# Attention and two feed-forward layers on one core: the second group's sums moved to VectorE, value products by two chunks of keys, and new planning numbers

## Chip, cores and metric

One core of a Trainium2 chip runs the whole kernel. The metric is the time of one execution on the device, in microseconds (us); the value given for a kernel is the median of several runs. Engines are named as the profile names them: PE is TensorE (PEld its loading of weights), DVE is VectorE, ACT is ScalarE, POOL is GpSimd, SP is SyncE, which issues the transfers.

## What is computed

Everything is float32. Four batches of 12 heads, 448 positions, 64 numbers a head; then two feed-forward layers over the 1792 rows that the heads give.

```python
q_n, k_n = rmsnorm(q, g_q), rmsnorm(k, g_k)
scores = (q_n @ k_n.T) / sqrt(64)
attn = exp(scores - max(scores)); attn = attn / (sum(attn) + 1e-9)
x = (attn @ v), heads side by side            # 1792 x 768
x = ((x @ w_a) * (x @ w_b)) @ w_out           # 768 -> 1536 -> 768
h = x @ w_in                                  # 768 -> 2048
out = (h * clip(h + 3, 0, 6) / 6) @ w_out2    # 2048 -> 768
```

## The kernel before

**Precision.** A large product is made of three: each operand is split into a high part, rounded to the fast type `float32r` by ACT, and a low part, the difference, made by DVE or POOL (`sub`, line 397). `tri` (line 690) issues high x high, high x low and low x high. The products of 448 columns at lines 691 to 693 (first group) and 964 (second group) are nearly all of PE's work.

**Attention** works on pairs of heads (`pair`, line 418). Scores come in seven chunks of 128 queries (lines 533 and 534), are reduced and exponentiated into seven tiles `p`, and are transposed back by blocks (lines 571, 585 to 588) into a buffer `pt`, of which there are two. The keys have four chunks for a pair of heads; for each chunk `k` one value step (`value`, line 596, product at 598) multiplies the transposed block with v for both heads and adds into one PSUM bank. Chunk 3 holds the last 64 keys of both heads, so its operands have another shape than those of chunks 0 to 2.

**Feed-forward** is done in two groups of two batches. The first group (batches 0 and 1) runs through `layer` while attention of batches 1 to 3 goes on beside it, to about 790 us in the profile. Weights are unpacked there by DVE and split by ACT and by POOL or DVE (`piece`, line 663). The second group (batches 2 and 3) runs through `layer7` (line 878), twice, once for each layer. It cuts each product of matrices into 2 x 2 blocks and needs seven block products instead of eight, at the price of sums: sums of weight blocks (`Left.sum`, line 921), the low parts of weights (`halve`, line 896), sums of activation blocks and their low parts (`Right`, line 1024), and the gate of the first layer (`gate`, line 1011). Results are added up out of PSUM by DVE (`take`, line 968). `x_maker` (line 826) prepares the activations at the start of either layer.

**The order of the work** is planned when the program is built. Each operation is added with a due time in a planned clock and with the engines that may do it, each with an estimated duration (`Plan.add`, line 166). `Plan.run` goes through planned time: each free engine takes the operation that is due first and whose inputs and buffers are there; one that may go to a second engine goes there if the first is busy for longer than `LW` or the operation is late. So the numbers at the top of the file set the order: `T` and `TQ` place the batches of attention, `R` the start and pace of each feed-forward layer, `O*` the offsets inside a pair of heads, `LW7`, `LX7`, `XLEAD`, `XSTEP` those of the second group, `LB`, `LF`, `LW` when an operation may go to another engine. On the chip each engine runs its own list in order and waits where an input is late.

```python
        vg, gv = {"V": (on_dve(PH), True), "G": on_pool(PH)}, {"G": on_pool(PH), "V": (on_dve(PH), True)}
            add(at(u + OD[1]), {"PE": 930}, value, reads=[(pt, 0), (pt, 1), rv], writes=[pv])
```

The first line (885) lets weight sums of the second group go to DVE ("V") or POOL ("G"), each with its cost in ns; the second (601) adds one value step.

Of the kernel before, what the change touches and what calls it, by code (L numbers as in the profile page):

```python
# [19 lines left out]
NB, NH, S, D = 4, 12, 448, 64  # L20
# [5 lines left out]
PH = DM // 2  # L26
# [1 line left out]

T = (6.793, 78.0, 255.0, 440.0)
TQ = (1.45, 3.637, 4.75, 4.118)
R = ((85.0, 1.515), (255.0, 1.267), (411.278, 1.34), (703.581, 1.0), (943.0, 1.0))


BS = ((2, 3, 4), (1, 2, 3, 4), (2, 3, 4), (3, 4))
# [18 lines left out]

LB = (
    (548.658, 276.261, 561.206), (548.658, 402.965, 561.206), (548.658, 402.965, 561.206),
    (735.919, 402.965, 561.206),  # L60
)
LF = (
    (548.658, 402.965, 561.206), (548.658, 402.965, 561.206), (548.658, 402.965, 561.206),
    (548.658, -149.766, 561.206),
)
LW = 112.877


OA = (-7.027, -5.631, -5.6, -5.526, -4.903, -4.8, -4.475, -4.381)
OB = (-4.0, -2.7, -3.2, -2.3, -2.579, -2.6, -2.385)  # L70
OC = (0.0, -0.24, 0.482, 0.457, 4.632, 4.519)
UT = 5.13
UK = 2.0
OD = (0.4, 1.972, 3.0)


LEAD = 21.868
OW = (-9.089, -9.23, 1.129, 3.002, -1.607)
AFTER = 2.571


SLICE = (3, 3, 2)
# [4 lines left out]


MM = 206.7
LW7 = (34.0, 25.0, 20.0, 18.0)  # L90

SLICE7 = ((3, 3), (3, 3, 2))
XLEAD, XSTEP = -14.0, 3.7
LX7 = (20.0, 19.0, 18.5)


def piece_order(up, down, n, k):
# [49 lines left out]
class Plan:  # L149
# [16 lines left out]
    def add(self, due, cost, fn, reads=(), writes=(), after=()):  # L166


        o = Op()
        o.due, o.fn, o.idx = due * 1000.0, fn, len(self.ops)  # L170
        o.late = self.late
        o.cost = {e: c if isinstance(c, tuple) else (c, e == "G") for e, c in cost.items()}
        o.succ, o.need, o.ready = [], 0, 0.0
        o.bufs = []
        deps = {id(d): d for d in after}
        for k in reads:
            if k in self.last:
                deps[id(self.last[k])] = self.last[k]
        for k in writes:
            if k in self.last:  # L180
                deps[id(self.last[k])] = self.last[k]
            for d in self.readers.pop(k, ()):
                deps[id(d)] = d
        for k in reads:
            self.readers.setdefault(k, []).append(o)
        for k in writes:
            self.last[k] = o
        seen = set()
        for k in (*reads, *writes):
            b = k[0] if isinstance(k, tuple) else k  # L190
            if isinstance(b, Buf) and id(b) not in seen:
                seen.add(id(b))
                o.bufs.append(b)
                b.left += 1
        deps.pop(id(o), None)
        for d in deps.values():
            d.succ.append(o)
        o.need = len(deps)
        self.ops.append(o)
        return o  # L200
# [103 lines left out]
def on_dve(n):  # L304
    return 66 + 1.043 * n
# [4 lines left out]


def on_pool(n):
    return (146 + 2.11 * n, True)


@with_exitstack
def fused_kernel(ctx: ExitStack, tc: tile.TileContext, nat, qt, gs_in, wpk, outT):
    nc = tc.nc
    V, A, G, SP = nc.vector, nc.scalar, nc.gpsimd, nc.sync
# [11 lines left out]
    def f32(ap):  # L331
        return ap.bitcast(F32)
# [57 lines left out]
    def bank(role, ids, ordered=True):  # L390
        return Buf([banks[i] for i in ids], lines.setdefault(role, []) if ordered else None)

    plan = Plan()
    add = plan.add

    def sub(e, out, a, b):
        e.tensor_tensor(out=out, in0=a, in1=b, op=ALU.subtract)  # L397
# [20 lines left out]
    def pair(n0):  # L418
# [6 lines left out]
        lower, upper = slice(0, D), slice(D, P)  # L425

        def at(u):
            return t0 + q * u

        def at_chunk(j):  # L430
# [4 lines left out]
        rn, rv, sq, kc, ms, rstd, nt, sums, rs = [  # L435
            buf(k) for k in ("rn", "rv", "sq", "kc", "ms", "rstd", "nt", "sums", "rs")]
# [5 lines left out]
        for i, (lo, hi, who) in enumerate(alike):  # L442
            add(at(-10.7 + i), {"SP": 90 * (hi - lo)}, lambda e, lo=lo, hi=hi: e.dma_start(
                out=rn.t[:, lo:hi].rearrange("p c d -> p (c d)"), in_=nat[n0 // 2][:, lo * D:hi * D]),
                writes=[(rn, k) for k in who])
        for i in range(2):
            add(at(-8.9 + (4 * i if n0 else 0)), {"SP": 640}, lambda e, i=i: e.dma_start(out=rqs[i].t, in_=qt[n0 + i]),
                writes=[rqs[i]])
        add(at(-2.0), {"SP": 640}, lambda e: e.dma_start(
            out=rv.t.rearrange("p c d -> p (c d)"), in_=nat[n0 // 2][:, 14 * D:]), writes=[rv])  # L450
        for i, (lo, hi, who) in enumerate(alike):
            n, sl = (hi - lo) * D, slice(lo, hi)
            x, y, z, m, sk = [[(o, k) for k in who] for o in (rn, rstd, nt, ms, sq)]

            def square(e, sl=sl):
# [5 lines left out]
            cost = {"V": (on_dve(n), True), "A": on_act(n), "G": on_pool(n)}  # L461
            add(at(OA[0]), {k: cost[k] for k in ("VAA"[i] if n0 == 0 else SQ[b])}, square,
                reads=x, writes=sk)
            add(at(OA[1]), {"V": on_dve(n)}, lambda e, sl=sl: e.reduce_sum(out=ms.t[:, sl], in_=sq.t[:, sl], axis=AX.X),
                reads=sk, writes=m)
# [3 lines left out]
                reads=m, writes=y)  # L469
            add(at(OA[4]), {"A": 100}, lambda e, sl=sl: e.activation(rstd.t[:, sl], rstd.t[:, sl], AF.Exp, scale=-0.5),  # L470
                writes=y)
# [85 lines left out]
        for j in range(0 if LATE[b] else NCK):  # L557
            opts = {"V": (363, True), "G": (617, True), "A": 560}
            add(at(4 + OC[5] + 0.15 * j), {k: opts[k] for k in NORM[b][j // 2]}, lambda e, j=j: norm(e, j),
                reads=[rs], writes=[ps[j]])  # L560
        pv = bank("v", BV[b])
        for k in range(4):
            pt = buf("pt")
            u = 4 + UT + k * UK
            if k < 3:
                for i, n in enumerate((4, 3)):
                    t = bank("t", BT[b], False)

                    def turn_p(e, k=k, i=i, n=n, t=t):
                        for c in range(n):  # L570
                            e.transpose(t.t[:, c * P:(c + 1) * P], ps[4 * i + c].t[:, k * P:(k + 1) * P], ident)  # L571

                    add(at(u + 0.5 * UK * i), {"PE": 109 * n}, turn_p, writes=[t, (pt, i)],
                        reads=["ident", *ps[4 * i:4 * i + n]])
                    cost = copy_ps(n * P)
                    add(at(u + 0.5 * UK * i + OD[0]), {x: cost[x] for x in PT[b]}, lambda e, i=i, n=n, t=t, pt=pt: copy(
                        e, pt.t[:, 4 * P * i:(4 * i + n) * P], t.t[:, :n * P]), reads=[t], writes=[(pt, i)])
                own = slice(0, P), slice(0, P)
                at_v, cols = (k, 4 + k), (0, S)
            else:  # L580
                t = bank("t", BT[b], False)

                def turn_rest(e, t=t):
                    for c in range(4):
                        e.transpose(t.t[:, c * P:(c + 1) * P], ps[3 + c].t[:, S - P:], ident)
                    for c in range(3):
                        e.transpose(t.t[lower, c * P:(c + 1) * P], ps[c].t[:, S - D:], ident)  # L587
                    e.transpose(t.t[lower, 3 * P:S], ps[3].t[lower, S - D:], ident[lower, lower])

                add(at(u), {"PE": 820}, turn_rest, reads=["ident", *ps], writes=[t, (pt, 0)])  # L590
                cost = copy_ps(4 * P)
                add(at(u + OD[0]), {x: cost[x] for x in PT[b]}, lambda e, t=t, pt=pt: copy(
                    e, pt.t[:, :4 * P], t.t), reads=[t], writes=[(pt, 0)])
                own, at_v, cols = (lower, upper), (3, 3), (0, D)

            def value(e, k=k, pt=pt, own=own, at_v=at_v, cols=cols):
                for i, rows in enumerate((lower, upper)):
                    e.matmul(pv.t[rows, :S], rv.t[own[i], at_v[i]], pt.t[own[i], cols[i]:cols[i] + S],  # L598
                             start=k == 0, stop=k == 3)

            add(at(u + OD[1]), {"PE": 930}, value, reads=[(pt, 0), (pt, 1), rv], writes=[pv])
        m, due = h // 2, at(u + OD[2])
        if LATE[b]:
            rb, eb = bank("t", BT[b], False), buf("tmp", "e")
# [273 lines left out]
    def layer7(no, ids, clock, late, finish):  # L878
# [3 lines left out]
        n = LAYERS[no][2] // 2  # L882
        now = dict(sevens)
        sevens.clear()
        vg, gv = {"V": (on_dve(PH), True), "G": on_pool(PH)}, {"G": on_pool(PH), "V": (on_dve(PH), True)}

        def mbank():
            return bank("m", ids)
# [120 lines left out]
            return t  # L1009

        def gate(c, ap, due, in_psum, b):
            cost = {"V": 535} if in_psum else {"V": (535, True), "G": on_pool(S)}
            add(due, cost, lambda e: e.tensor_tensor(out=b.t, in0=ap(), in1=b.t, op=ALU.mult), reads=[c], writes=[b])
            return b

# [8 lines left out]
        class Right:  # L1024
# [6 lines left out]
            def __call__(self, name, due):  # L1031
                x11, x12, x21, x22 = self.x
                if name == "t1":
                    self.minus(x12, x12, x11, due - LX7[0])
                if name == "t3":
                    self.minus(x11, x22, x11, due - LX7[0])
                c = {"b11": x11, "t1": x12, "b22": x22, "b21": x21, "t2": x22, "t3": x11, "t4": x21}[name]
                a = buf("act")
                add(due - LX7[1], {"A": 467}, lambda e: e.activation(a.t[:, 0], c.t, AF.Copy), reads=[c], writes=[(a, 0)])
                add(due - LX7[2], {"V": (535, True), "G": on_pool(S)}, lambda e: sub(e, a.t[:, 1], c.t, f32(a.t[:, 0])),  # L1040
                    reads=[c, (a, 0)], writes=[(a, 1)])
                if name == "b22":
                    self.minus(x22, x22, x12, due - LX7[2])
                if name == "b21":
                    self.minus(x21, x21, x22, due - LX7[2])
                return a

            def minus(self, to, x, y, due):
                add(due, {"V": (535, True), "G": on_pool(S)}, lambda e: sub(e, to.t, x.t, y.t),
                    reads=[z for z in (x, y) if z is not to], writes=[to])  # L1050

        def down(pairs, first, last):
# [128 lines left out]
```

## Time and profile before

| | |
|---|---|
| median of 3 runs | 1277.68 us (1277.48 to 1277.71) |
| the profiled execution | 1274.44 us |
| its span, first to last instruction | 1272.7 us |
| PE busy | 1236.0 us (97%) |
| DVE busy | 1027.8 us (81%) |
| ACT busy | 668.9 us (53%) |
| POOL busy | 258.0 us (20%) |

The profile records one execution. The 1.7 us between the profiled execution and its span lie before the first and behind the last instruction. Times inside the trace count from the start of the span. A matmul in the trace is shown with a modelled end, and consecutive ones overlap; the cost of one is read from start to start.

### The profile page before, as it was taken

To read this page: it belongs to the slowest core of one execution; us is meant where nothing else is said; L and a number is where in the kernel's file an instruction comes from. 1 tells how busy PE (TensorE), PEld (TensorE's weight loads), DVE (VectorE), ACT (ScalarE), POOL (GpSimd) and SP (SyncE) were. 2 spreads that over 40 slices of the span, in tenths; PEclk is the share of its full clock that TensorE was granted. 3 is DMA by queue.
4 is the path that set the end of the run, shared out by engine and by line. 5 is a ranking of instruction groups with operands and counts; after the bars stand their busy time and mean duration, and the time that the engine had idled before them with its cause. 6 is when DMAs were issued, how large, how long until landed. Compare 5 with 4: busy or idle time off the path is not lost.

```text
span 1272.7 us, 18366 instructions
## 1 busy us (share of the span) xinstructions
PE 1236.0 (97%) x6342; PEld 1039.3 (82%) x6342; DVE 1027.8 (81%) x1859; ACT 668.9 (53%) x1428; POOL 258.0 (20%) x281
## 2 busy tenths in 40 slices
PE   5999999999999999999999999999999999899998
PEld 3668777777988887888778878899899888799897
DVE  8999998997557798877878775876877799977977
ACT  7996766677235564654767643522422245534432
POOL 4331102212000021110121000522212234413131
PEclk9999999999999999999999999999999999999999
DMA  6456676765687587656646353655355445255433
GB/s 203 139 187 227 215 257 203 281 228 197 216 274 241 173 314 252 207 177 227 205 142 209 122 173 108 232 155 162 121 176 158 132 129 182 85 178 157 131 107 123
DMA packets 107853, 235.57 MB, mean 185 GB/s; under 512 B 9200, under 2 KB 74096, under 8 KB 107760
## 3 DMA queue, kind: packets, MB, share of 16 engines
q1 hardware_dynamic: 107760, 234.39, 56.2%
q8 instruction: 50, 0.82, 0.3%
q14 instruction: 43, 0.35, 0.1%
HBM read 162.01 MB, written 72.35 MB: 184 GB/s over the span
## 4 chain that ended last, share of the span: by engine, by line
PE 73%; DVE 15%; DMA 5%; issue 4%; ACT 2%; POOL 1%; SPq 0%; DVEq 0%; POOLq 0%; ACTq 0%
PE bank L964 26%; PE bank L691 10%; PE bank L693 10%; PE bank L692 10%; PE bank L598 5%; PE bank L571 4%; DMA wst<-in_w_dram 3%; PE bank L533 3%; PE bank L534 2%; DVE act L397 2%; DVE w L397 2%; DMA rn<-in_nat_dram 1%; PE bank L498 1%; DVE wf L649 1%; DVE acc L972 1%
## 5 line engine op out<-in xcount | busy, mean ns | idle before, releaser
L691 PE MATMUL bank<-xx,w 128*128 128x448 f32 x480 | 182.3, 380 | 1.1 <-DVE act L397 0.9
L693 PE MATMUL bank<-xx,w 128*128 128x448 f32 x480 | 175.5, 366 | 0.0
L692 PE MATMUL bank<-xx,w 128*128 128x448 f32 x480 | 175.4, 365 | 0.0
L964 PE MATMUL bank<-act,w 128*128 128x448 f32 x711 | 155.0, 366 | 6.0 <-DVE acc L972 4.1
L964 PEld LDWEIGHTS bank<-act,w 128*128 128x128 f32 x711 | 133.0, 188 | 18.9 <-ACT w L899 4.4
L964 PE MATMUL bank<-xx,w 128*128 128x448 f32 x612 | 132.1, 366 | 0.8 <-DVE acc L972 0.8
L691 PE MATMUL bank<-act,w 128*128 128x448 f32 x336 | 127.7, 380 | 2.6 <-DVE act L397 1.9
L673 ACT ACTIVATE w<-wf 128x768 fp32r<-128x768 f32 x104 | 85.6, 840 | 78.9 <-PE bank L692 64.8
L964 PEld LDWEIGHTS bank<-xx,w 128*128 128x128 f32 x612 | 114.9, 188 | 10.8 <-DVE acc L972 1.2
L693 PE MATMUL bank<-act,w 128*128 128x448 f32 x336 | 122.8, 366 | 0.0
L692 PE MATMUL bank<-act,w 128*128 128x448 f32 x336 | 122.7, 365 | 0.0
L397 DVE TENSOR_TENSOR w<-wf,w 128x384 fp32r<-128x384 f32 x185 | 101.3, 584 | 18.9 <-ACT w L673 15.8
L797 DVE TENSOR_TENSOR acc<-bank,acc 128x448 f32<-128x448 f32 x120 | 74.3, 622 | 48.4 <-PE bank L693 48.0
L539 DVE TENSOR_REDUCE nm<-bank 128x1 f32<-128x448 f32 x168 | 102.4, 618 | 13.0 <-PE bank L534 8.3
L543 ACT ACTIVATE p<-bank,nm,rstd 128x448 f32<-128x448 f32 x131 | 94.5, 724 | 27.5 <-PE bank L587 17.0
L408 ACT ACTIVATE pt<-bank 128x512 f32<-128x512 f32 (+1 forms) x131 | 71.4, 547 | 61.7 <-PE bank L571 51.4
L397 POOL TENSOR_TENSOR w<-wf,w 128x384 fp32r<-128x384 f32 x48 | 55.0, 1154 | 230.4 <-ACT w L673 224.8
L691 PEld LDWEIGHTS bank<-xx,w 128*128 128x128 f32 x480 | 90.2, 188 | 12.6 <-DVE act L397 1.7
L693 PEld LDWEIGHTS bank<-xx,w 128*128 128x128 f32 x480 | 90.1, 188 | 7.7
L692 PEld LDWEIGHTS bank<-xx,w 128*128 128x128 f32 x480 | 90.4, 188 | 6.2
L598 PE MATMUL bank<-pt,rv 128*64 128x448 f32 (+1 forms) x384 | 92.5, 563 | 0.5 <-DVE act L397 0.5
L964 PE MATMUL bank<-xt,w 128*128 128x448 f32 x405 | 89.7, 368 | 3.1 <-DVE xf L412 3.1
(214 smaller groups left out, 2487.4 us busy)
## 6 DMA issues: line engine op xcount, KB each, us to landing
wst<-in_w_dram SPq DMA_DIRECT2D x68, 768.0 KB, 5.9
split<-w SPq DMA_DIRECT2D x102, 384.0 KB, 3.7
w<-split SPq DMA_DIRECT2D x85, 384.0 KB, 3.9
kept<-wf SPq DMA_DIRECT2D x68, 384.0 KB, 3.0
wf<-kept SPq DMA_DIRECT2D x65, 384.0 KB, 4.2
wst<-kept SPq DMA_DIRECT2D x39, 384.0 KB, 3.6
rq<-in_qt_dram SPq DMA_DIRECT2D x48, 224.0 KB, 3.4
rn<-in_nat_dram SPq DMA_DIRECT2D x23, 448.0 KB, 4.1
```

What stands on the lines that cost most here:

```text
L397: e.tensor_tensor(out=out, in0=a, in1=b, op=ALU.subtract)
L408: A.activation(out, in_, AF.Copy)
L539: add(at(u + OC[1]), {"V": 531}, lambda e, s=s, nm=nm: e.tensor_reduce(out=nm.t, in_=s.t[:, :S], axis=AX.X, op=ALU.max, negate=True), read ...
L543: add(at(u + OC[3]), {"A": 704}, lambda e, j=j, s=s, nm=nm, p=p: e.activation(p.t, s.t[:, :S], AF.Exp, bias=nm.t, scale=rstd.t[:, qcol[j]: ...
L571: e.transpose(t.t[:, c * P:(c + 1) * P], ps[4 * i + c].t[:, k * P:(k + 1) * P], ident)
L598: e.matmul(pv.t[rows, :S], rv.t[own[i], at_v[i]], pt.t[own[i], cols[i]:cols[i] + S], start=k == 0, stop=k == 3)
L673: add(due - LEAD + OW[2], {"A": on_act(DM)}, lambda e: e.activation(w.t[:, 0], wf.t.bitcast(F32), AF.Copy), reads=both, writes=[(w, 0, 0), ...
L691: e.matmul(ps, w.t[:, 0, wsl], xh, start=start, stop=False)
L692: e.matmul(ps, w.t[:, 0, wsl], xl, start=False, stop=False)
L693: e.matmul(ps, w.t[:, 1, wsl], xh, start=False, stop=stop)
L797: add(due, {"V": 535}, lambda e, m=m, bi=bi, ps=ps: e.tensor_tensor(out=acc[:, m, bi], in0=ps.t[:, :S], in1=acc[:, m, bi], op=ALU.add), re ...
L964: e.matmul(out, w.t[:, a, chunk(c)], x, start=first and j + k == 0, stop=j + k == n + 1, skip_group_check=not first)
```

## The change

Four things change. In `pair`, `value` now collects the chunks and is added once for two of them (0 and 1, 2 and 3): two steps' products stand back to back and wait for both blocks. In `layer7`, the weight sums, low parts, activation sums and the gate have only DVE as their engine. `Plan.add` counts each DVE operation 3% longer, and `on_pool` counts large POOL operations 25% longer. And most offsets at the top get new values, of which two lines stand here.

```diff
-T = (6.793, 78.0, 255.0, 440.0)
-TQ = (1.45, 3.637, 4.75, 4.118)
-R = ((85.0, 1.515), (255.0, 1.267), (411.278, 1.34), (703.581, 1.0), (943.0, 1.0))
+T = (6.793, 74.014, 253.235, 440.0)
+TQ = (1.436, 3.637, 4.788, 4.218)
+R = ((85.0, 1.761), (255.0, 1.223), (411.278, 1.34), (703.581, 1.0), (932.169, 1.0))
...
-LX7 = (20.0, 19.0, 18.5)
+LX7 = (10.733, 19.0, 18.5)
...
+        if "V" in o.cost:
+            o.cost["V"] = o.cost["V"][0] * 1.03, o.cost["V"][1]
...
 def on_pool(n):
-    return (146 + 2.11 * n, True)
+    return ((146 + 2.11 * n) * (1.25 if n >= PH else 1.0), True)
...
         pv = bank("v", BV[b])
+        pts = []
         for k in range(4):
...
-            def value(e, k=k, pt=pt, own=own, at_v=at_v, cols=cols):
-                for i, rows in enumerate((lower, upper)):
-                    e.matmul(pv.t[rows, :S], rv.t[own[i], at_v[i]], pt.t[own[i], cols[i]:cols[i] + S],
-                             start=k == 0, stop=k == 3)
-
-            add(at(u + OD[1]), {"PE": 930}, value, reads=[(pt, 0), (pt, 1), rv], writes=[pv])
+            pts.append((k, pt, own, at_v, cols))
+            if k % 2 == 0:
+                continue
+
+            def value(e, two=tuple(pts)):
+                for k, pt, own, at_v, cols in two:
+                    for i, rows in enumerate((lower, upper)):
+                        e.matmul(pv.t[rows, :S], rv.t[own[i], at_v[i]], pt.t[own[i], cols[i]:cols[i] + S],
+                                 start=k == 0, stop=k == 3)
+
+            add(at(u + OD[1]), {"PE": 1750}, value, reads=[rv, *((t[1], x) for t in pts for x in range(2))], writes=[pv])
+            pts = []
...
-        vg, gv = {"V": (on_dve(PH), True), "G": on_pool(PH)}, {"G": on_pool(PH), "V": (on_dve(PH), True)}
+        vg = gv = {"V": (on_dve(PH), True)}
...
-            cost = {"V": 535} if in_psum else {"V": (535, True), "G": on_pool(S)}
+            cost = {"V": 535} if in_psum else {"V": (535, True)}
...
-                add(due - LX7[2], {"V": (535, True), "G": on_pool(S)}, lambda e: sub(e, a.t[:, 1], c.t, f32(a.t[:, 0])),
+                add(due - LX7[2], {"V": (535, True)}, lambda e: sub(e, a.t[:, 1], c.t, f32(a.t[:, 0])),
...
-                add(due, {"V": (535, True), "G": on_pool(S)}, lambda e: sub(e, to.t, x.t, y.t),
+                add(due, {"V": (535, True)}, lambda e: sub(e, to.t, x.t, y.t),
```

Three places in the order of the instructions show it. Lines are those of each kernel's own file (the change's stand three or so lower or higher); x2 behind a row means two such instructions.

PE, first chunks of a pair of heads in batch 1, before; `bank_70` is the value step's bank, `pt_273` and `pt_274` the two transposed blocks, `p` and `ident` belong to transposes, `xx,w` to projection products:

```order
L693 MATMUL bank_63<-xx,w_239 128x448
L598 MATMUL bank_70<-pt_273,rv_256 64x448 x2
L571 MATMUL bank_68<-ident,p_268 128x128
L571 MATMUL bank_68<-ident,p_269 128x128
L571 MATMUL bank_68<-ident,p_270 128x128
L571 MATMUL bank_68<-ident,p_266 128x128
L691 MATMUL bank_63<-xx,w_239 128x448
```

The same place after the change (here the other buffer of v):

```order
L529 MATMUL bank_64<-kk_265,qh_261 128x448
L530 MATMUL bank_64<-kk_265,ql_263 128x448
L600 MATMUL bank_70<-pt_273,rv_257 64x448 x2
L600 MATMUL bank_70<-pt_274,rv_257 64x448 x2
L694 MATMUL bank_65<-xx,w_237 128x448
```

The steps of two chunks stand together, and no block of transposes follows them directly.

POOL, in the last layer of the second group, before: weight sums (L922), low parts (L397) of weights (`w`, `wb`) and of an activation (`act`):

```order
L922 TENSOR_TENSOR wst_232<-wst_232 128x384
L397 TENSOR_TENSOR w_238<-wst_233,w_238 128x384
L922 TENSOR_TENSOR wst_232<-ws_6819,wst_232 128x384
L922 TENSOR_TENSOR ws_6821<-wst_233,wf_234 128x384
L922 TENSOR_TENSOR wf_236<-ws_6820,wf_236 128x384
L922 TENSOR_TENSOR wst_233<-wst_233 128x384
L397 TENSOR_TENSOR act_241<-xf,act_241 128x448
```

POOL's last rows after the change, which are those of `x_maker` at the start of the last layer:

```order
L393 TENSOR_TENSOR xx<-acc,xx 128x448 x2
L393 TENSOR_TENSOR acc<-acc 128x448 x2
L393 TENSOR_TENSOR xt_6855<-acc,xt_6855 128x448
L393 TENSOR_TENSOR acc<-acc 128x448
L393 TENSOR_TENSOR xt_6857<-acc,xt_6857 128x448
L393 TENSOR_TENSOR xt_6858<-acc,xt_6858 128x448
```

Behind these POOL has nothing more to do; the sums stand on DVE.

PE, where the first layer of the second group ends and the last layer begins, before; `act` products close the one, `xx` products open the other:

```order
L964 MATMUL bank_63<-act_241,wb_6817 128x448 x3
L964 MATMUL bank_63<-act_242,w_237 128x448 x3
L964 MATMUL bank_63<-act_243,w_238 128x448 x3
L964 MATMUL bank_65<-act_241,wb_6817 128x448 x3
L964 MATMUL bank_65<-act_242,w_237 128x448 x3
L964 MATMUL bank_65<-act_243,w_238 128x448 x3
L964 MATMUL bank_64<-act_241,wb_6817 128x448 x3
L964 MATMUL bank_64<-act_242,w_237 128x448 x3
L964 MATMUL bank_64<-act_243,w_238 128x448 x3
L964 MATMUL bank_63<-xx,w_238 128x448 x9
```

And after the change:

```order
L967 MATMUL bank_66<-xx,w_238 128x448 x9
L967 MATMUL bank_63<-act_241,wb_6859 128x448 x3
L967 MATMUL bank_63<-act_242,w_237 128x448 x3
L967 MATMUL bank_63<-act_243,w_238 128x448 x3
L967 MATMUL bank_67<-xx,w_237 128x448 x9
L967 MATMUL bank_64<-act_241,wb_6859 128x448 x3
L967 MATMUL bank_64<-act_242,w_237 128x448 x3
L967 MATMUL bank_64<-act_243,w_238 128x448 x3
L967 MATMUL bank_63<-xx,w_239 128x448 x9
```

Three opening products now stand among the last three closing ones.

## Rows read from the trace of the kernel before

**Rows 1.** The page: span, then busy us, share and instructions of each engine.

```profile
span 1272.7 us, 18366 instructions
PE 1236.0 (97%) x6342; PEld 1039.3 (82%) x6342; DVE 1027.8 (81%) x1859; ACT 668.9 (53%) x1428; POOL 258.0 (20%) x281
```

**Rows 2.** Busy time by stretch: length, engines' busy us (instructions), PE clock, DMA.

```profile
core 0: us, PE busy (x) PEld busy (x) DVE busy (x) ACT busy (x) POOL busy (x), PEclk, DMA share, GB/s
20.00:85.00 65.00, 62.78 (x421) 40.33 (x419) 62.66 (x125) 60.94 (x164) 28.05 (x45) 1.00 0.51 159
85.00:255.00 170.00, 167.31 (x883) 132.00 (x883) 156.25 (x293) 117.50 (x257) 28.11 (x37) 1.00 0.69 234
255.00:785.00 530.00, 526.92 (x2730) 431.80 (x2729) 400.58 (x746) 298.20 (x630) 60.02 (x75) 1.00 0.61 207
785.00:1000.00 215.00, 212.86 (x1042) 193.88 (x1041) 158.33 (x271) 68.52 (x133) 51.13 (x43) 1.00 0.52 160
1000.00:1105.00 105.00, 95.67 (x457) 86.47 (x456) 100.10 (x151) 49.62 (x97) 48.12 (x39) 0.98 0.43 132
1105.00:1273.00 168.00, 161.85 (x795) 148.71 (x794) 134.70 (x233) 63.22 (x122) 37.17 (x31) 1.00 0.44 137
...
1060.00:1100.00 40.00, 35.61 (x167) 32.12 (x166) 37.73 (x58) 19.84 (x38) 20.56 (x18) 0.96 0.49 154
1074.00:1087.00 13.00, 11.72 (x58) 10.53 (x58) 12.68 (x14) 6.57 (x13) 11.46 (x10) 1.00 0.60 182
```

**Rows 3.** Timeline of PE around a single value step: start us, us, instruction.

```profile
127.71 0.36 PE L693 MATMUL bank<-xx,w 128*128 128x448 f32 x1
128.00 0.97 PE L598 MATMUL bank<-pt,rv 128*64 128x448 f32 x4
128.90 0.66 PE L571 MATMUL bank<-ident,p 128*128 128x128 f32 x4
129.31 0.45 PE L691 MATMUL bank<-xx,w 128*128 128x448 f32 x1
129.60 0.36 PE L692 MATMUL bank<-xx,w 128*128 128x448 f32 x1
```

**Rows 4.** Timeline of PE where two steps stand together, at 678 and 72 us.

```profile
678.09 0.37 PE L693 MATMUL bank<-xx,w 128*128 128x448 f32 x1
678.38 1.72 PE L598 MATMUL bank<-pt,rv 128*64 128x448 f32 x8
680.04 0.66 PE L571 MATMUL bank<-ident,p 128*128 128x128 f32 x4
...
71.72 0.36 PE L534 MATMUL bank<-kk,ql 128*128 128x448 f32 x1
72.01 1.87 PE L598 MATMUL bank<-pt,rv 128*64 128x448 f32 x8
73.81 0.47 PE L533 MATMUL bank<-kk,qh 128*128 128x448 f32 x1
```

**Rows 5.** Timeline of PE, the two longest waits of the second group, in brackets.

```profile
1025.42 1.46 PE L964 MATMUL bank<-act,w 128*128 128x448 f32 x6 [2.47 <-DVE acc L972]
...
1091.62 2.70 PE L964 MATMUL bank<-xt,w 128*128 128x448 f32 x9 [3.10 <-DVE xf L412]
```

**Rows 6.** Timelines of POOL (first row) and of DVE, 1078 to 1090 us.

```profile
1078.48 1.40 POOL L922 TENSOR_TENSOR wf<-ws,wf 128x384 f32<-128x384 f32 x1
...
1078.94 1.43 DVE L1020 SCALAR_TENSOR_TENSOR tmp<-tmp,tmpx 128x448 f32<-128x448 f32 x1
...
1088.42 0.61 DVE L972 TENSOR_TENSOR tmpx<-bank,tmpx 128x448 f32<-128x448 f32 x1
1088.96 0.54 DVE L922 TENSOR_TENSOR ws<-wf,wst 128x384 f32<-128x384 f32 x1
1089.42 0.55 DVE L922 TENSOR_TENSOR ws<-wst,wf 128x384 f32<-128x384 f32 x1
```

**Rows 7.** The page's costliest groups, two: busy us, mean ns of one, idle before.

```profile
L408 ACT ACTIVATE pt<-bank 128x512 f32<-128x512 f32 (+1 forms) x131 | 71.4, 547 | 61.7 <-PE bank L571 51.4
...
L397 POOL TENSOR_TENSOR w<-wf,w 128x384 fp32r<-128x384 f32 x48 | 55.0, 1154 | 230.4 <-ACT w L673 224.8
```

More of the change, by code (lines that the diff above doesn't have):

```diff
@@ L54 @@
 LATE = (True, False, False, False)
[L58 to L71, printed above, removed]
+LB = ((344.344, 276.261, 381.127), (548.658, 402.965, 561.206), (548.658, 402.965, 561.206), (606.623, 311.013, 561.206))
+LF = ((548.658, 376.129, 761.141), (548.658, 402.965, 561.206), (548.658, 402.965, 561.206), (553.891, -149.766, 668.974))
+LW = 161.162
+OA = (-7.027, -5.631, -5.6, -5.311, -5.026, -4.8, -4.475, -4.381)
+OB = (-4.77, -2.7, -3.245, -2.3, -2.091, -2.6, -2.386)
+OC = (0.104, -0.677, 0.482, 0.457, 4.632, 4.519)
 UT = 5.13
@@ L74 @@
 OD = (0.4, 1.972, 3.0)
-LEAD = 21.868
-OW = (-9.089, -9.23, 1.129, 3.002, -1.607)
-AFTER = 2.571
+LEAD = 22.604
+OW = (-8.493, -9.23, 1.129, 3.002, -1.61)
+AFTER = 2.346
 SLICE = (3, 3, 2)
@@ L89 @@
 MM = 206.7
-LW7 = (34.0, 25.0, 20.0, 18.0)
+LW7 = (26.748, 25.0, 15.217, 11.821)
 SLICE7 = ((3, 3), (3, 3, 2))
-XLEAD, XSTEP = -14.0, 3.7
-LX7 = (20.0, 19.0, 18.5)
+XLEAD, XSTEP = -11.077, 4.422
+LX7 = (10.733, 19.0, 18.5)
 def piece_order(up, down, n, k):
```

## The prediction

> **What bounds the kernel now.** I read four views in this order. The busy times of the page come first: TensorE (PE) is busy for 97% of the span, VectorE (DVE) for 81%, and GpSimd (POOL) runs 281 instructions [rows 1]. A kernel with PE at 97% can gain in two ways only: shorter work on PE, or the few holes closed. The table by stretch says where the holes are [rows 2]. From 85 to 785 us PE is idle for 2.7 + 3.1 us in 700, so there only PE's own work counts. From 20 to 85 us it is idle for 2.2 us. From 785 us on, about where the second group begins, it is idle for 2.1 us up to 1000 us, for 9.3 us from 1000 to 1105 us, and for 6.2 us after that, of which the last 3 or 4 us are the output leaving. From 1000 to 1105 us DVE is busy for 100.1 of 105 us: this one stretch belongs to DVE.
>
> The timeline of PE shows the price of one value step and of two that stand back to back [rows 3, 4]. The timeline of the late stretch shows what PE waited for: 2.47 us before 1025.42 and 3.10 us before 1091.62, both for DVE to empty or copy a bank [rows 5]. DVE and POOL side by side show why DVE is late there [rows 6].
>
> **Part 1, two chunks of keys in one value step.** In the order every one of the 96 value steps becomes half of a pair: 48 merged steps. Before, six pairs already stand back to back by chance: two of chunks 0 and 1, four of chunks 2 and 3. So 22 pairs of the first kind and 20 of the second are new.
>
> A single step [rows 3]: the product before it starts at 127.71, the step at 128.00, the next instruction at 128.90. That is 1.19 us from start to start, of which the earlier product needs its own 0.20; the step costs 0.99, and two cost 1.98. Chunks 0 and 1 back to back [rows 4]: from 678.09 to 680.04, 1.95 - 0.20 = 1.75, so 0.23 is saved. Chunks 2 and 3: from 71.72 to 73.81, 2.09 - 0.20 = 1.89, so 0.09 is saved (chunk 3 has another tile shape). Together 22 x 0.23 + 20 x 0.09 = 6.9 us of PE.
>
> Something goes back. Most single steps handed PE straight to a block of transposes; now many blocks of transposes stand alone. A return from either kind to 448-column products costs 0.09 more than the usual 0.20 (129.31 to 129.60, [rows 3]), and by the order the returns rise from 162 to 175: 1.2 us. That leaves 5.7. I take **-5 us**, since some steps stood directly behind transposes and entered cheaper than [rows 3]. Bounds: -6.9, and 0 if the merged step waits for its second half (below). Nearly all of it lies where PE has no holes, so it should come out of the span one to one.
>
> What the merge delays: both `pt` buffers are held until the merged step is done, so the copies of the next two chunks start later, and behind them the next value step. From 85 us on PE has projection products to put in between; the order shows them there. Before 85 us it has little; that is a rival below.
>
> **Part 2, the sums of the second group.** By the order some 93 sums of POOL (about 67 of 384 elements, 26 of 448) go to DVE. A sum costs DVE 0.46 us (384 elements, 1088.96 to 1089.42) or 0.54 (448, 1088.42 to 1088.96) from start to start [rows 6]: 67 x 0.46 + 26 x 0.54 = 45 us more work. Against it stands what POOL does to DVE. At 1078.48 POOL starts a sum of 1.40 us, and the DVE instruction at 1078.94 takes 1.43 us instead of the 0.62 of its size [rows 6]. In the 13 us from 1074 to 1087 DVE is busy for 12.68 us with 14 instructions, where eleven of 0.54 and three of 0.46, two of them cut by the window, would need about 7; POOL does ten sums in that time [rows 2]. So ten sums on POOL cost DVE some 5.7 us of blocking; done by DVE itself they cost 9 x 0.46 + 0.54 = 4.7. Where DVE is full, POOL's help is worth nothing, or a little less.
>
> The Trainium skill ("SBUF — State Buffer", Who interferes with whom) says that a DVE instruction with two inputs in SBUF contends with a GpSimd instruction that reads SBUF, and that the one which issues second is blocked. The trace agrees: 1.43 us instead of 0.62. By that rule alone the exchange is about even, as summed here.
>
> Where does that leave each stretch? From 785 to 1000 us, 43 POOL instructions: even with no relief DVE goes to at most 158 + 43 x 0.5 = 180 of 215. After 1105 us, 31: at most 150 of 168. Neither becomes the bound. From 1000 to 1105 us, 39: 39 x 0.48 = 19 us more and, at 0.57 a sum, up to 22 less: DVE stays at 95 to 100 of 105, about where it is. The gain must therefore come from latency and from the order. A sum in the chain takes 0.5 instead of 1.0 to 1.4 us and hands over within one engine. The last layer's clock starts 10.8 us earlier (943.0 to 932.169), so that work moves into the stretch before 1000 us, where DVE has a quarter free; and in the new order three products of the next layer stand among the last three of the layer before it, where nothing stood, so that a late bank has cover.
>
> The idle time to win is 2.1 + 9.3 + about 2.5 = 14 us. I add the clock: from 1060 to 1100 us the granted clock is 0.96, after the long wait [rows 2, 5], some 1.5 us. Of these 15 us I expect about half: **-7 us**. Bounds: -15 (every hole closed) and +18 (no relief, all of 39 x 0.48 on a full DVE).
>
> **Part 3, the rest.** 27 more weight splits of the first group go to POOL (48 to 75). One takes 1.15 us there [rows 7], where DVE would be free again after 0.46 [rows 6]. Weights come well ahead of PE there: it loses 3.1 us in 530 [rows 2]. Without that cover each such piece would come about 0.7 us later. The plan's higher costs (VectorE by 3%, large POOL sums by 25%) and the other offsets change due times only; SP issues 567 transfers in both, and nothing of theirs ends a wait in [rows 5]. I cost this at 0, between -2 and +3, since PE is idle for 8 us in all from 20 to 785.
>
> **The sum.** The profiled execution took 1274.44 us, 3.24 below the median of the runs, 1277.68. 1274.44 - 5 - 7 = 1262.4; set on the median, 1277.68 - 12 = **1266 us**. A measurement of this kernel tells about 0.2% (2.6 us) from no change, so faster means under 1275.1 and slower above 1280.3.
>
> **Rivals.**
> - *All late holes close.* The blocked chains vanish and the order is good: 1277.7 - 5 - 15 = 1258. For it: every late wait ends with DVE. Against it: DVE stays at 95% in the stretch.
> - *The exchange is a wash.* DVE as full as before from 1000 to 1105 us, the holes stay and merely change place: 1277.7 - 5 = 1273. For it: 19 us added, up to 22 taken off.
> - *The merged step starves the first 85 us.* Twelve merged steps there wait for the copy of the second chunk; one copy is 0.55 us [rows 7], so up to 6.6 us: 1277.7 - 5 - 7 + 6.6 = 1272; with the wash 1279. For it: PE, DVE and ACT are all over 90% there [rows 2]. Against it: the order puts scores between.
> - *DVE becomes the bound of the second group (slower).* If the long DVE instructions are long for another reason than POOL, the 39 sums of 1000 to 1105 us lie on an engine that has 5 us free. It decides from the point where relief is under about 14 us: with 10, 1277.7 - 5 + 9 = 1282; with none, 1291. Against it: the long ones lie beside POOL's sums and the short ones do not [rows 6]. The Trainium skill ("Perfetto Trace Analysis", Optimizing Scalar/DVE Operations) says that a saturated DVE may be worth relieving by GpSimd, and adds that their shared port may spoil it. By its first half this change is a step back and this rival holds; the trace bears out the second.
>
> **The numbers.** Forecast (1261 to 1271): 0.50. All holes close (1257 to 1261): 0.12. Wash (1271 to 1275.1): 0.17. Starved start (1270 to 1279): 0.09. DVE bound (over 1279): 0.12. Faster: 0.50 + 0.12 + 0.17 + a third of 0.09 = 0.82; same 0.06; slower 0.12. The range leaves out most of the DVE case and the edge below: 1258 to 1277.
>
> **What would show it.** Right: merged steps at 1.66 and 1.80 us, no PE wait of a microsecond on them; in the second group no DVE instruction of 448 elements over 0.65 us after the last POOL sum; PE idle from 1000 to 1105 us about halved. Wrong: DVE busy for all of that stretch with PE waiting as long as before (wash) or longer (DVE bound); PE idle in 20 to 85 us well over 2.2 us (starved start).

## The result, and the profile after

| | before | after |
|---|---|---|
| median | 1277.58 us (4 runs, 1272.8 to 1277.71) | 1256.99 us (4 runs, 1254.26 to 1258.03) |
| ratio to before | | 0.9843, 95% interval 0.9827 to 0.986 |
| span of the profiled execution | 1272.7 us | 1254.4 us |
| first product of the second group starts at | 816.6 us | 813.7 us |
| from there to the start of its last product | 451.7 us | 436.9 us |

The change is faster by 20.6 us. The forecast was 1266 us, with 1258 as the lower end, so the time lies just outside the range. Of the 18.3 us between the two spans, 14.9 lie in the second group, and 3.0 before it.

The page and the table by stretch of the changed kernel, in the form of [rows 1] and [rows 2] (length, then busy us and instructions of PE, PEld, DVE, ACT and POOL, then PE clock):

```profile
span 1254.4 us, 18336 instructions
PE 1228.4 (98%) x6342; PEld 1046.4 (83%) x6342; DVE 1031.7 (82%) x1906; ACT 673.3 (54%) x1422; POOL 197.5 (16%) x240
```

```profile
20.00:85.00 65.00, 63.38 (x420) 43.47 (x421) 59.52 (x121) 62.88 (x166) 28.64 (x50) 1.00 0.51 169
85.00:255.00 170.00, 169.79 (x926) 137.07 (x925) 158.88 (x289) 123.95 (x271) 48.63 (x59) 1.00 0.65 223
255.00:785.00 530.00, 528.05 (x2737) 439.12 (x2737) 396.83 (x722) 297.48 (x618) 81.41 (x94) 1.00 0.61 210
785.00:1000.00 215.00, 210.91 (x1022) 192.83 (x1021) 168.85 (x303) 66.36 (x130) 20.62 (x16) 0.98 0.52 163
1000.00:1105.00 105.00, 103.13 (x505) 94.17 (x504) 103.85 (x190) 56.52 (x110) 14.49 (x11) 1.00 0.43 137
1105.00:1255.00 150.00, 145.88 (x720) 134.84 (x718) 128.72 (x241) 56.05 (x105) 0.00 (x0) 1.00 0.45 143
```

From 1000 to 1105 us PE was idle for 9.3 us before and is idle for 1.9 now, although DVE is fuller than ever there: 103.85 of 105 us. From 785 to 1000 us it is the other way round: 2.1 us idle before, 4.1 now, and the clock is at 0.98. The list of PE's waits from 785 us to the end has three lines, and the first is new (who waited, for what, total us, times, longest). The other two, 1.9 us, are all that PE waits inside the second group; before, it waited there for 11.9 us.

```profile
PE bank L694 <- DVE acc L800: 4.1, 2, 2.3
PE bank L967 <- DVE acc L975: 1.2, 2, 1.0
PE bank L967 <- ACT xf L404: 0.7, 1, 0.7
```

**The new hole** lies where the first group ends. PE, DVE and POOL side by side (start us, us, instruction), and the stretch in the form of [rows 2]:

```profile
795.62 0.47 PE L694 MATMUL bank<-act,w 128*128 128x448 f32 x1 [1.82 <-DVE acc L800]
...
797.05 0.58 PE L696 MATMUL bank<-act,w 128*128 128x448 f32 x1
797.42 0.58 PE L694 MATMUL bank<-act,w 128*128 128x448 f32 x1
...
805.84 0.47 PE L694 MATMUL bank<-act,w 128*128 128x448 f32 x1 [2.26 <-DVE acc L800]
...
789.32 2.87 DVE L925 TENSOR_TENSOR ws<-wst 128x384 f32<-128x384 f32 x2
792.11 1.51 DVE L925 TENSOR_TENSOR wst<-wf,wst 128x384 f32<-128x384 f32 x1
...
794.95 0.61 DVE L800 TENSOR_TENSOR acc<-bank,acc 128x448 f32<-128x448 f32 x1
...
802.34 1.51 DVE L925 TENSOR_TENSOR ws<-wf 128x384 f32<-128x384 f32 x1
803.77 1.48 DVE L925 TENSOR_TENSOR ws<-wst 128x384 f32<-128x384 f32 x1
...
789.18 4.03 POOL L393 TENSOR_TENSOR xf<-xf 128x448 f32<-128x448 f32 x3
797.22 7.62 POOL L393 TENSOR_TENSOR xx<-xf,xx 128x448 fp32r<-128x448 f32 x6 [4.01 <-ACT xx L711]
```

```profile
795.00:805.00 10.00, 7.96 (x30) 6.89 (x30) 7.97 (x11) 2.46 (x5) 7.70 (x7) 0.83 0.25 92
```

Before 795.62 PE waits for the addition at 794.95 (L800), which empties a bank of the first group's last products. In DVE's list weight sums of the second group (L925) stand ahead of it, and three of these take about 1.45 us instead of 0.54, beside three differences of `x_maker` on POOL. Before 805.84 it is the same: two weight sums of 1.5 us on DVE, beside splits of `x_maker` on POOL. This looks like the blocking of [rows 6] in a new place; a run below tests it. After each wait about ten products start 0.37 us apart instead of 0.20 (797.05 to 797.42). The granted clock is 0.83 in these 10 us, so part of them runs at 1.2 instead of 2.4 GHz. The two waits cost 4.1 us, and the slow products, some 20 x 0.17, another 3.4.

**The merged steps**, in the form of [rows 4]:

```profile
142.03 0.37 PE L696 MATMUL bank<-act,w 128*128 128x448 f32 x1
142.32 1.87 PE L600 MATMUL bank<-pt,rv 128*64 128x448 f32 x8
144.13 0.47 PE L529 MATMUL bank<-kk,qh 128*128 128x448 f32 x1
...
155.33 0.37 PE L530 MATMUL bank<-kk,ql 128*128 128x448 f32 x1
155.63 1.72 PE L600 MATMUL bank<-pt,rv 128*64 128x448 f32 x8
157.28 0.47 PE L694 MATMUL bank<-xx,w 128*128 128x448 f32 x1
```

From one neighbour to the other they take 2.10 and 1.95 us, as the two pairs of [rows 4] did. PE waits at none of the 48 merged steps.

**DVE in the second group**, groups of instructions from 830 us on (count, busy us, mean ns of one):

```profile
L393 DVE TENSOR_TENSOR act<-xf,act 128x448 fp32r<-128x448 f32 x56 | 35.5, 651 | 0.1
L393 DVE TENSOR_TENSOR w<-ws,w 128x384 fp32r<-128x384 f32 x51 | 27.6, 548 | 0.0
...
L393 DVE TENSOR_TENSOR act<-tmpx,act 128x448 fp32r<-128x448 f32 x25 | 15.3, 616 | 0.0
```

Two of the three groups are at the plain duration of their size, 548 and 616 ns; the first holds two that still fall beside `x_maker`, of 1.58 us each. After POOL's last instruction, which ends at 1067.4 us, no DVE instruction of 448 elements takes more than 0.63 us.

### The profile page after: what moved, and what is told of

The parts are those of the page before. It is cut to its first block, busy times and chain, and to the rows that moved or that the text cites. A ratio compares the mean times of both kernels' runs of the same rounds, so it can differ in the third digit from the quotient of the medians.

```text
span 1254.4 us, 18336 instructions
## 1 busy us (share of the span) xinstructions
PE 1228.4 (98%) x6342; PEld 1046.4 (83%) x6342; DVE 1031.7 (82%) x1906; ACT 673.3 (54%) x1422; POOL 197.5 (16%) x240
## 4 chain that ended last, share of the span: by engine, by line
PE 84%; DVE 9%; DMA 3%; ACT 2%; issue 1%; SPq 0%; DVEq 0%; POOL 0%; ACTq 0%
PE bank L967 30%; PE bank L694 12%; PE bank L696 11%; PE bank L695 11%; PE bank L600 6%; PE bank L568 4%; PE bank L529 3%; PE bank L530 3%; DMA wst<-in_w_dram 2%; PE bank L494 1%; DVE act L393 1%; DVE acc L975 1%; PE bank L582 1%; DVE wf L655 1%; DVE w L393 1%
## 5 line engine op out<-in xcount | busy, mean ns | idle before, releaser
L967 PEld LDWEIGHTS bank<-act,w 128*128 128x128 f32 x711 | 133.5, 188 | 10.6
L393 POOL TENSOR_TENSOR w<-wf,w 128x384 fp32r<-128x384 f32 x75 | 81.5, 1099 | 254.8 <-ACT w L676 240.3
L800 DVE TENSOR_TENSOR acc<-bank,acc 128x448 f32<-128x448 f32 x120 | 74.3, 620 | 51.3 <-PE bank L696 50.7
L393 DVE TENSOR_TENSOR w<-wf,w 128x384 fp32r<-128x384 f32 x158 | 87.4, 587 | 13.4 <-ACT w L676 10.7
L600 PE MATMUL bank<-pt,rv 128*64 128x448 f32 (+1 forms) x384 | 86.2, 557 | 0.0
## 6 DMA issues: line engine op xcount, KB each, us to landing
rn<-in_nat_dram SPq DMA_DIRECT2D x23, 448.0 KB, 4.2
```

The lines of the kernel that those rows point to most:

```text
L800: add(due, {"V": 535}, lambda e, m=m, bi=bi, ps=ps: e.tensor_tensor(out=acc[:, m, bi], in0=ps.t[:, :S], in1=acc[:, m, bi], op=ALU.add), re ...
L967: e.matmul(out, w.t[:, a, chunk(c)], x, start=first and j + k == 0, stop=j + k == n + 1, skip_group_check=not first)
```

## The experiments

Two questions were open: which part of the change closed the holes of the second group, and where the 3 us before it come from. Four kernels first, each with some of the parts. In all tables "start" is the start of the second group's first product in the profiled execution, and "length" the time from there to the start of its last one. The ratio is to runs of the kernel before taken beside each batch; their medians were 1276.09 us for the first four kernels, 1277.54 for the next three and 1276.88 for the last three.

**Merge alone**, the kernel before with the new `value`:

```diff
...
+            add(at(u + OD[1]), {"PE": 1750}, value, reads=[rv, *((t[1], x) for t in pts for x in range(2))], writes=[pv])
...
```

> The kernel before with the value products merged by two chunks of keys and nothing else; all planning numbers and the POOL sums as before. Theory: the merge shortens PE's work by about 7 us in the first 815 us wherever the rest is put, so 1271 (1268 to 1274), with the second group still about 452 us long from its first product to its last and its waits for DVE still there. Rival (the merge needs the new offsets): the second chunk is late, PE waits in front of merged steps, and the time is 1275 or more.

**Sums alone**, the kernel before with the engine lists of the second group cut to DVE:

```diff
+        vg = gv = {"V": (on_dve(PH), True)}
...
+            cost = {"V": 535} if in_psum else {"V": (535, True)}
...
```

> The kernel before with the sums of the second group on DVE alone; planning numbers and single value steps as before. Theory A (POOL's sums block DVE, and the holes of the second group come from that): the second group shrinks from 452 us to about 440, the time to 1265 (1262 to 1268). Rival B (the new numbers close the holes): the second group stays at 448 to 460 us, the time 1275 or more.

**Numbers alone**, the changed kernel with both of these undone:

> The changed kernel with single value steps and with the sums of the second group open to POOL again: what is left is the new numbers and the new costs of the plan. Theory A: second group still 448 us or longer, time 1272 to 1280. Rival B: second group about 438 us, time about 1264.

**Merge and numbers**, the changed kernel with the sums open to POOL again:

```diff
-        vg = gv = {"V": (on_dve(PH), True)}
+        vg, gv = {"V": (on_dve(PH), True), "G": on_pool(PH)}, {"G": on_pool(PH), "V": (on_dve(PH), True)}
...
```

> The changed kernel with the sums of the second group open to POOL again, merge and numbers kept. Theory A: the second group goes back to 447 to 455 us and the time to 1269 (1265 to 1274). Rival B: the second group stays at 437 to 441 us and the time within 3 us of the change, 1254 to 1260.

| | median | ratio to before, interval | start | length |
|---|---|---|---|---|
| merge alone | 1271.34 | 0.9963 (0.995 to 0.9975) | 812.8 | 451.6 |
| sums alone | 1268.58 | 0.9948 (0.9929 to 0.9967) | 816.6 | 444.8 |
| numbers alone | 1270.68 | 0.9966 (0.9938 to 0.9994) | 818.1 | 445.5 |
| merge and numbers | 1259.59 | 0.9873 (0.9858 to 0.9887) | 806.3 | 448.0 |

Neither theory holds alone. The sums take 6.9 us off the length, the numbers without them 6.2, both together 14.9 (the change). The merge leaves the length alone and acts on the start: 3.8 us with the old numbers, 11.8 with the new (818.1 to 806.3). With merge and numbers, and the sums on POOL, there is no hole at 800 us, which is why this kernel came some 5 us below the least that theory A gave. Beside it the sums on DVE win about 11 us in the second group and lose 7 just before it. Without the merge the same exchange (numbers alone against the kernel without the merge, below) wins 8.5 and loses 3.7.

The hole does not belong to the moved sums alone. The kernel with the numbers alone, where POOL still takes sums, has it too: PE waits twice for the same addition, 3.7 us in all. So of the 11.8 us between that kernel and merge and numbers, 3.7 are a hole that closed.

With the sums alone, PE idle from 1000 to 1105 us falls from 9.3 to 4.4; with the numbers alone to 1.8, although POOL still runs 38 instructions in that stretch (the first row is that of the sums, the second that of the numbers):

```profile
1000.00:1105.00 105.00, 100.58 (x485) 90.11 (x484) 102.39 (x188) 55.99 (x110) 12.02 (x9) 1.00 0.43 136
1000.00:1105.00 105.00, 103.23 (x503) 93.63 (x502) 98.11 (x161) 56.03 (x110) 47.91 (x38) 1.00 0.44 139
```

**Three kernels on the hole, the merge and the blocking itself.** In the first, `x_maker` loses POOL as well:

```diff
-            vg = {"V": (535, True), "G": on_pool(S)}
+            vg = {"V": (535, True)}
...
-                split(at(name), (hi, lo), src[:, m, bi], [key(m, bi), *hold((m, bi))], out, "VG")
+                split(at(name), (hi, lo), src[:, m, bi], [key(m, bi), *hold((m, bi))], out, "V")
```

> The changed kernel with the last POOL work around the second group, the splits and differences of x_maker, on DVE alone too. Theory C (the new hole of the change at 793 to 806 us, 4.1 us of waiting and some 3 us of slower matmuls, comes from x_maker's work on POOL stretching the weight sums that are now on DVE): the hole closes, the second group starts at 806 to 808 us, time about 1250 (1248 to 1253). Rival (DVE simply has too much to do there, whoever does x_maker): the hole stays or grows by the added work, time 1257 to 1263.

The second is the changed kernel with single value steps again:

> The changed kernel with single value steps again. Theory: the merge is worth about 7 us in any order, time 1264 (1261 to 1267). Rival (the new offsets were made for the merge, and without it the first 800 us lose more): 1268 or more. The run with numbers alone and the one with numbers and merge lay 11 us apart, which speaks for the rival.

The third gives POOL idle sums, beside an unchanged order on the other engines:

```diff
...
+                if after_us:
+                    d = buf("spare")
+                    add(self.first - LW7[1] + after_us + 0.1, {"G": (1, False)}, lambda e: [e.tensor_tensor(
+                        out=d.t, in0=out[0]()[:, c:c + PH // 2], in1=out[0]()[:, c:c + PH // 2], op=op)
+                        for c in (0, PH // 2)], reads=out[1], writes=[d], after=ends)
```

> The changed kernel with 102 additional sums on POOL in the second group, each in two halves of 192 elements, that read a weight sum and write a tile nobody reads; the order on PE, DVE and ACT is that of the change. Theory A (a sum on POOL blocks DVE): DVE instructions with two inputs in SBUF grow again beside them, DVE gets fuller from 1000 to 1105 us, the second group goes from 437 to 443 us or more, time 1261 to 1268. Rival B (only the order and the numbers count, POOL disturbs nobody): time within 2 us of 1257.

| | median | ratio to before, interval | start | length |
|---|---|---|---|---|
| x_maker on DVE too | 1246.43 | 0.9761 (0.974 to 0.9782) | 804.1 | 436.6 |
| no merge | 1267.28 | 0.9925 (0.9898 to 0.9952) | 821.9 | 436.9 |
| idle sums on POOL | 1267.21 | 0.9919 (0.9892 to 0.9946) | 807.1 | 456.6 |

`x_maker` on DVE closes the hole. At the same place DVE has the same weight sums, now short, and the addition comes in time:

```profile
787.51 1.02 DVE L925 TENSOR_TENSOR ws<-wst 128x384 f32<-128x384 f32 x2
788.44 0.55 DVE L925 TENSOR_TENSOR wst<-wf,wst 128x384 f32<-128x384 f32 x1
...
790.80 0.62 DVE L800 TENSOR_TENSOR acc<-bank,acc 128x448 f32<-128x448 f32 x1 [0.40 <-PE bank L696]
```

```profile
785.00:1000.00 215.00, 215.00 (x1060) 197.84 (x1060) 177.19 (x335) 68.05 (x133) 0.00 (x0) 1.00 0.53 166
```

The sums take 0.55 us or less each, DVE now waits for PE at 790.80, and PE is busy for all of 215 us. At 1246.43 us this is the fastest kernel of the study, 10.6 us below the change; it gained more than the 7 us expected, and the second group did not get longer although DVE took over all of POOL's work there.

Without the merge the start comes 8.2 us later (821.9 against 813.7) at the same length. The merge is worth 8 to 12 us with the new numbers, and about 4 to 5 with the old. A part of this difference is holes. Up to the start of the second group PE is busy for 795.8 us before and for 791.4 with the merge alone, and 1.7 of these are lost where the granted clock is 0.83 from 148 to 158 us: 6.1 us less work. With the new numbers it is 797.17 without the merge (numbers alone) and 788.74 with it (merge and numbers): 8.4 us less.

The idle sums show the blocking. PE, DVE and ACT have the change's order, nothing needs the results of the idle sums, and yet the second group is 19.7 us longer; its some 700 DVE instructions take 21 us longer in sum. DVE and POOL near 1085 us, then the stretch:

```profile
1084.57 0.86 DVE L393 TENSOR_TENSOR wb<-ws,wb 128x384 fp32r<-128x384 f32 x1
1085.35 0.86 DVE L925 TENSOR_TENSOR ws<-wf,wst 128x384 f32<-128x384 f32 x1
1086.13 0.86 DVE L925 TENSOR_TENSOR ws<-wst,wf 128x384 f32<-128x384 f32 x1
...
1085.09 3.11 POOL L930 TENSOR_TENSOR spare<-wst 128x192 f32<-128x192 f32 x4
```

```profile
1000.00:1105.00 105.00, 95.57 (x440) 85.01 (x439) 96.16 (x167) 49.48 (x96) 46.46 (x49) 0.95 0.41 128
```

DVE's steps come 0.78 us apart instead of 0.46, in time with POOL's halves of 0.78. PE's idle time is back at 9.4 us. DVE did not get fuller in this stretch, as was expected; it gets through fewer instructions, 167 against 190.

Not all of the 19.7 us is blocking of DVE. `x_maker` still has instructions on POOL, and the idle sums stand ahead of some of them there. PE's longest wait comes from POOL being late: ACT waits 4.97 us for a difference of `x_maker`, and the copy that PE needs stands behind it in ACT's list.

```profile
1050.24 1.48 POOL L930 TENSOR_TENSOR spare<-wst 128x192 f32<-128x192 f32 x2
...
1052.85 2.22 POOL L393 TENSOR_TENSOR acc<-acc 128x448 f32<-128x448 f32 x2
...
1054.01 0.58 ACT L871 ACTIVATE xt<-acc 128x448 fp32r<-128x448 f32 x1 [4.97 <-POOL acc L393]
...
1056.83 7.36 PE L972 MATMUL bank<-xx,w 128*128 128x448 f32 x27 [3.61 <-ACT tmpx L404]
```

With the clock behind it (0.83 from 1055 to 1065 us, 1.7 us lost) this is some 5 us of the 19.7. The idle sums also hold buffers up to a microsecond longer, so a little more may be theirs. The time rose by 10.2 us and not by 20, because the hole at 800 us happened to be smaller in this kernel (PE waits 2.1 us there, and the clock holds), start 807.1.

**Three kernels on the numbers.** All moves to DVE and the merge, with the old numbers and costs:

> The kernel before with the merge, the sums of the second group on DVE and x_maker on DVE, but all its own planning numbers and costs. Theory (the numbers have a share of their own, in the second group by 6 us and in the first by letting the merge save more): the second group is about 443 to 445 us long, its start lies at 812 us, time 1260 (1256 to 1264), clearly above the 1246 of the same kernel with new numbers. Rival (with nothing left on POOL there the numbers do not matter): within 4 us of 1246.

The changed kernel with one number put back:

```diff
-R = ((85.0, 1.761), (255.0, 1.223), (411.278, 1.34), (703.581, 1.0), (932.169, 1.0))
+R = ((85.0, 1.761), (255.0, 1.223), (411.278, 1.34), (703.581, 1.0), (943.0, 1.0))
```

> The changed kernel with the last layer's planned start put back from 932.169 to 943.0, nothing else. Theory D (the earlier start moves the last layer's sums into the stretch where DVE is free and gives PE cover): the stretch from 1030 to 1110 us gets its holes back, second group 441 to 446 us, time 1261 to 1266. Rival (the shorter leads LW7 and LX7 or the costs do it): second group stays at 436 to 439 us, time 1255 to 1259.

And with the leads of the second group put back:

```diff
-LW7 = (26.748, 25.0, 15.217, 11.821)
+LW7 = (34.0, 25.0, 20.0, 18.0)
...
-XLEAD, XSTEP = -11.077, 4.422
-LX7 = (10.733, 19.0, 18.5)
+XLEAD, XSTEP = -14.0, 3.7
+LX7 = (20.0, 19.0, 18.5)
```

> The changed kernel with the leads of the second group (LW7, LX7, XLEAD, XSTEP) put back, the start at 932.169 kept. Theory D: second group stays at 436 to 440 us, time 1255 to 1260. Rival (the leads do it): sums and low parts are planned too early, crowd DVE's list ahead of what PE waits for, second group 441 us or more, time 1261 or more.

| | median | ratio to before, interval | start | length |
|---|---|---|---|---|
| all on DVE, old numbers | 1261.91 | 0.9896 (0.9874 to 0.9918) | 810.1 | 442.9 |
| last start 943 | 1252.97 | 0.9816 (0.9801 to 0.9832) | 811.6 | 436.3 |
| old leads | 1261.88 | 0.9885 (0.9865 to 0.9905) | 811.8 | 443.6 |

Theory D falls: the earlier start of the last layer is worth nothing (436.3 against 436.9). With the number put back the kernel is even 4.0 us faster by the medians, 2.1 of them before the second group; why was not found. The leads are the numbers' share: 6.7 us of length. With the old leads PE waits 4.8 us in the second group instead of 1.9. The longest wait, in the last layer, is for a copy that empties a bank, as at 1091.62 in [rows 5]. Behind it lies a stretch at a lower clock:

```profile
1076.12 2.54 PE L967 MATMUL bank<-xt,w 128*128 128x448 f32 x9 [2.17 <-ACT xf L404]
```

```profile
1076.00:1086.00 10.00, 9.21 (x31) 7.77 (x32) 8.15 (x17) 4.58 (x10) 0.00 (x0) 0.66 0.29 102
```

A granted clock of 0.66 over 10 us means that PE runs at 1.2 instead of 2.4 GHz for about 6.8 of them, and that costs 3.4 us. So about half of what the leads are worth is the clock behind this one wait.

By the new leads, activations' sums (`LX7`, 20 to 10.7 us ahead) and weights' (`LW7`) are due later, so less of what is not yet needed stands in DVE's list ahead of what empties banks. That the order of the list is the way by which the leads act was not shown by itself; nor which of the four settings matters most.

The old numbers cost 15.5 us in all (1261.91 against 1246.43): 6.3 in the second group and 6.0 before it; the rest lies between two medians and two single profiles.

## Why the prediction was wrong, step by step

- **What bounds the kernel**: right. PE stays at 97 to 98%, and all that was won is shorter work on PE or closed holes.
- **Part 1, the merge, -5**: right in its mechanism, and in its size for the old order. The pairs cost 1.75 and 1.90 above a neighbour, as [rows 4] gave, and nothing starves: PE idle from 20 to 85 us went from 2.2 to 1.6. The merge alone took 4.8 us off the time and 6.1 off PE's work, where the sum had 5.7 and I took 5. In the new order it is worth more: 8.2 us of start, 8.4 of work. That the size would hang on the order I did not see. What I left out: the transposes too get cheaper. Summed from start to start over their rows up to the second group, without PE's waits, they take 75.1 us before and 72.5 with the merge alone.
- **Part 2, the exchange is even where DVE is full**: the blocking is shown, by the idle sums above all. The price of 0.57 us a sum holds where both engines are packed (0.32 for each half near 1085 us); over the whole second group the 102 idle sums cost DVE 21 us, 0.2 each. For the stretch from 1000 to 1105 us DVE at 95 to 100 of 105 was forecast and 103.85 came.
- **Part 2, about half of the 15 us, and Part 3, the other offsets at 0**: these are the steps that failed. With the sums alone Part 2 came out at its size: 6.9 us off the second group against 7, and 4.4 of the 9.3 us of holes left. But my reason for the rest to stay, a DVE at 95%, was none. DVE rose to 103.85 of 105 us, and PE's waits in the group still went from 11.9 us to 1.9: PE does not wait for a busy DVE but for one particular instruction. The other half went with the offsets, of which Part 3 said that they "change due times only", 0 between -2 and +3. By themselves the new numbers took 6.2 us off the second group (5.4 off the time), and the change loses 6.7 us of length without the new leads. Together it was 14.9 us, all that I had counted.
- **The first rival, all late holes closed at 1258 us**, given 0.12, is what happened in that group. That the whole time came within 1 us of it is in part luck. Before the group it counts 5 us, all from the merge; 3.0 came there, from a larger merge and the other numbers, less a new hole of 7.5.
- **Part 2, the last layer's earlier start**: wrong. Put back, the length stays, although only one of the three opening products that I showed from the order then stands among the closing ones. So they decided nothing here.
- **Part 2, "Neither becomes the bound"**: right as an average, and blind to the new hole. I gave the stretch up to 1000 us "at most 180 of 215" on DVE. At its beginning, POOL's remaining work lengthens the weight sums that DVE now has to do ahead of the first group's last additions: a hole of 7.5 us, 9.6 in start against the kernel without it. It hid what the merge and the numbers won before it: merge and numbers start the second group at 806.3, the change at 813.7.
- **Part 3, more weight splits on POOL, at 0**: nothing speaks against it. PE idle from 255 to 785 us went from 3.1 to 2.0.
- **The DVE-bound rival** did not come: with all of POOL's work of the group on DVE, the kernel is faster still.

## What to carry to other kernels

Count what a helper engine's instruction costs the engine that it helps, from instructions of one size with and without it beside them; here, where both engines were packed, each cost about as much as it saved, and where both stood ahead of a bank's release they cost 7 to 10 us. When an engine is full, ask which instruction the bottleneck waits for and what stands ahead of it in the list: DVE at 99% left PE 1.9 us idle in 105, and in the largest hole DVE was just as busy, without a gap from 789.32 to 795.56, but on sums that nobody waited for yet. A busy share does not tell the two apart. Planning numbers deserve a term of their own in a forecast; here they were worth as much as the moved sums. After moving work, look at the edges of the stage, where the work left on the old engine meets it.

## What was not expected of the hardware

PE's products of 448 columns come at two steady distances, with the granted clock at 1.00 in both. With merge and numbers (sums on POOL), six products from 849.72 to 850.96, 206.7 ns each; in the changed kernel at the same time nine from 850.13 to 851.95, 202 ns each:

```profile
849.72 1.40 PE L967 MATMUL bank<-xt,wb 128*128 128x448 f32 x6
850.96 1.40 PE L967 MATMUL bank<-xx,wb 128*128 128x448 f32 x6
```

```profile
850.13 1.99 PE L967 MATMUL bank<-xt,w 128*128 128x448 f32 x9
851.95 0.36 PE L967 MATMUL bank<-xx,w 128*128 128x448 f32 x1
```

The slower one lasts from about 807 to 960 us in that kernel, and from about 840 to 898 us in the kernel before. In the kernel before it begins and ends at a wait of PE (0.04 and 0.70 us); with merge and numbers PE waits at neither end. At 2% it made that kernel's second group about 3 us longer, so its 448.0 should be read as about 445, and the 11 us that the sums win beside it as about 8. What sets it was not found: kernels with POOL idle show it too (the sums alone, from about 1095 to 1175 us).
